# Reordering the transposes and the loads at the end of a block: two chunks among an output block, the last chunk behind it and copied by VectorE, x loads behind the output store

## Chip, cores, metric

One core of a Trainium2 chip. The metric is device microseconds of one execution. TensorE is called PE in the profile, VectorE DVE, ScalarE ACT, GpSimd POOL, SyncE SP.

## The reference

A softmax over seven taps weights a causal window of tokens (a dynamic convolution, 8 heads, group 24); its output goes through a two-layer block with the activation h - tanh(h):

```python
w = exp(weight_gen - max); w = w / (sum(w) + 1e-9)          # (8, 4096, 8, 7)
x_unf = x_pad[:, arange(S)[:, None] + arange(7)[None, :]]    # window of 7 tokens
x = einsum('bshk,bskhg->bshg', w, x_unf)                     # -> 32768 x 192
h = x @ w_in                                                 # 192 -> 2048
out = (h - tanh(h)) @ w_out                                  # 2048 -> 192
```

## The kernel before

It works through 32 blocks of 1024 tokens in a software pipeline. In block n, TensorE runs the first GEMM of block n (16 "f tiles": `gemm1`), the second GEMM of block n - 1 (8 output blocks `gemm2`, one behind each pair of f tiles) and, at the end, the transposes of the convolution of block n + 1 (matmuls with an identity that also add the taps). ScalarE takes the tanh, VectorE the subtraction, GpSimd the products of the convolution. Chunks are the thirds of the 192 channels (0, 1 and the last, 2); two row tiles take one half of the block's tokens each; "dense transposes" are the stretch in which most of TensorE's instructions are transposes; the halo is the six tokens before a block that the window needs, zeros at the head of a sequence. The code is cut:

```python
psum_h = ... bufs=3      # three double banks, one ring, tag "ph": f tiles and transposes
obank  = two single banks of the second GEMM

def gemm1(n, f):                       # one f tile
    ph = psum_h.tile([P, 2, HT], ...)  # next buffer of the ring
    ... 3 x 2 matmuls, two row tiles ...
    last_act[0] = nc.scalar.activation(out=th[:], in_=ph_f, func=ACT.Tanh)
    last_sub[0] = nc.vector.tensor_sub(gt[:], ph_f, th[:])   # frees ph
# ...
for n in range(NTOT):
    if n + 3 < NTOT and n not in LATE:
        load_x(n + 3)                              # head of the block
    for p in range(J):
        gemm1(n, 2 * p); gemm1(n, 2 * p + 1)
        # ... softmax sums in three parts, p = 1..3; reciprocals p = 4, 5
        if p < 6 or n == NTOT - 1:
            gemm2((n - 1) * J + p)                 # p = 0 also stores block n - 2
        # ...
    # end of the block: last chunk among output block 6, the other two behind it
    sums = conv_sums(n + 1, ((2,),), pcs)
    def between(f):
        if LEAD <= f: some(sums, mix)
        if f == LEAD + J - 1: conv_out(n + 1, ((2,),), pcs)      # ScalarE
    gemm2((n - 1) * J + 6, between=between)
    conv(n + 1, (0, 1))                                          # ScalarE copy
    gemm2((n - 1) * J + 7, 0, FILL)
    softmax_norm(n + 3, pcs[0][:, 0])     # VectorE: small copy, scale, in the last chunk's bank
    gemm1(n, 14)
    gemm2((n - 1) * J + 7, FILL, HALF)
    gemm1(n, 15)
    gemm2((n - 1) * J + 7, HALF, NFT)
```

"Tile 14" below is f tile 14 of a block, "tile 1" f tile 1 of the next block.

The softmax here doesn't subtract the row's maximum and nothing guards it: scores larger than these inputs give would overflow.

Of the kernel before, what the change touches and what calls it, by code (L numbers as in the profile page):

```python
# [16 lines left out]
def kernel(  # L17
# [8 lines left out]
    nc = tc.nc  # L26

    B, S, D = x.shape
    H, K = weight_gen.shape[2], weight_gen.shape[3]
# [3 lines left out]
    R = P // 2  # L33
    HALO = K - 1

    J = 8
    TOK = P * J
    JH = J // 2
    HT = TOK // 2
    NSB = S // TOK  # L40
    NTOT = B * NSB
    NFT = F // P
# [32 lines left out]
    prods_of = {}  # L75
# [27 lines left out]
    def load_x(n, behind=None):  # L103
        b, s = divmod(n, NSB)
        s0 = s * TOK

        x_t = xpool.tile([P, HALO + J, D], FP32, name="x_t")

        def rows(p0, p1, r0=0, r1=HALO + J):
            first = x[0, 0:1]  # L110
            return nc.sync.dma_start(
                out=x_t[p0:p1, r0:r1, :],
                in_=bass.AP(
                    tensor=first.tensor,
                    offset=first.offset + (b * S + s0 + p0 * J - HALO + r0) * D,
                    ap=[[J * D, p1 - p0], [D, r1 - r0], [1, D]],
                ),
            )

        def no_halo():  # L120
            nc.sync.dma_start(
                out=x_t[0:1, 0:HALO, :],
                in_=zero[:].rearrange("o (h d) -> o h d", h=1).to_broadcast([1, HALO, D]),
            )


        if n == 0:
            rows(0, P, HALO, HALO + J)
            rows(16, P, 0, HALO)
            rows(1, 16, 0, HALO)  # L130
            no_halo()
        else:
            dma = rows(0, P)
            if behind is not None:
                order(dma, behind, "order of the loads")
            if s == 0:

                no_halo()
        x_of[n] = x_t
# [11 lines left out]
    def softmax_sum(n, j0=0, j1=J):  # L151

        if j0 == 0:
            zsum_of[n] = wgpool.tile([P, J * H], FP32, name="zsum")
        nc.vector.reduce_sum(  # L155
            out=zsum_of[n][:, j0 * H : j1 * H],
            in_=e_of[n][:, j0:j1].rearrange("p j h k -> p (j h) k"),
            axis=AX.X,
        )
# [91 lines left out]
    def conv_sums(n, parts, pcs, home=None):  # L251


        prods = prods_of[n]
        if n not in conv_of:
            conv_of[n] = cpool.tile([P, NC, HT], BF16, name="convT")
        for _ in parts:
            pcs.append(home or psum_h.tile([P, 2, HT], FP32, name="pc", tag="ph"))

        for gi in range(max(len(g) for g in prods)):  # L260
            for chunks, pc in zip(parts, pcs):
                some = [c for c in chunks if gi < len(prods[c])]
                last = gi == max(len(prods[c]) for c in chunks) - 1
                for c in some:
                    for j in range(JH):
                        col = ((c - chunks[0]) * JH + j) * R
                        for r in range(2):
                            nc.tensor.matmul(  # L268
                                pc[r][:, col : col + R] if home else pc[:, r, col : col + R],
                                lhsT=prods[c][gi][  # L270
                                    r * R : (r + 1) * R, c, 2 * j : 2 * j + 2
                                ].rearrange("p j h g -> p (j h g)"),
                                rhs=ident[r * R : (r + 1) * R, r * R : (r + 1) * R],
                                start=(gi == 0 and c == chunks[0] and j == 0),
                                stop=(last and c == some[-1] and j == JH - 1),
                            )
                            yield

    def conv_out(n, parts, pcs):
        for chunks, pc in zip(parts, pcs):  # L280
            c0, nch = chunks[0], len(chunks)
            out = conv_of[n][:, c0 : c0 + nch, :].rearrange("p c (j r t) -> p r (c j) t", r=2, t=R)
            cols = nch * JH * R
            if isinstance(pc, list):
                for r in range(2):
                    nc.scalar.activation(  # L286
                        out=out[:, r],
                        in_=pc[r][:, 0:cols].rearrange("p (cj t) -> p cj t", t=R),
                        func=ACT.Copy,
                    )  # L290
            else:
                last_conv[0] = nc.scalar.activation(  # L292
                    out=out,
                    in_=pc[:, :, 0:cols].rearrange("p r (cj t) -> p r cj t", t=R),
                    func=ACT.Copy,
                )

    def conv(n, *parts):
        pcs = []
        for _ in conv_sums(n, parts, pcs):  # L300
            pass
        conv_out(n, parts, pcs)

    def gemm1(n, f):
        convT = conv_of[n]
        ph = psum_h.tile([P, 2, HT], FP32, name="ph", tag="ph")
        for c in range(NC):
            for r in range(2):
                nc.tensor.matmul(  # L309
                    ph[:, r, :],  # L310
                    lhsT=w_in[r * R : (r + 1) * R, c, f * P : (f + 1) * P],
                    rhs=convT[r * R : (r + 1) * R, c, :],
                    start=(c == 0),
                    stop=(c == NC - 1),
                )
        th = tpool.tile([P, TOK], FP32, name="th")
        ph_f = ph[:].rearrange("p r t -> p (r t)")
        g1_act[0] = last_act.get(0)
        gt = gpool.tile([P, TOK], BF16, name=f"gt{f}", tag=f"gt{f}")
        last_act[0] = nc.scalar.activation(out=th[:], in_=ph_f, func=ACT.Tanh)  # L320
        last_sub[0] = nc.vector.tensor_sub(gt[:], ph_f, th[:])  # L321
        g_of.setdefault(n, []).append(gt)

    LAST = (NTOT - 1) * J
    LATE = (1, 2, 3)
    LEAD = 5
    FILL, HALF = 2, 9
    half = {}
    out_of = {}

# [139 lines left out]
    def some(sums, m):  # L470
        for _ in range(m):
            next(sums, None)

    load_wg(3)
    load_wg(4)
    for n in range(NTOT):
        if n + 3 < NTOT and n not in LATE:
            load_x(n + 3)
        for p in range(J):
            gemm1(n, 2 * p)  # L480
            gemm1(n, 2 * p + 1)
            if n == 0:


                if p == 3:
                    pcs = []
                    sums = conv_sums(1, ((0, 1),), pcs, obank)
                if 3 <= p <= 6:
                    some(sums, (3 if p == 3 else 1) * 4 * JH)
                if p == 7:  # L490
                    some(sums, K * 4 * JH)
                    conv_out(1, ((0, 1),), pcs)
                    conv(1, (2,))
                continue
            if p == 0 and n == 1:
                softmax_exp(3)
            if p == 1 and n == 1:
                softmax_norm_ramp(3)
                products(3)
            if n + 3 < NTOT:  # L500

                if p == 0:
                    softmax_exp(n + 3)
                if p == 0 and n + 4 < NTOT:
                    load_wg(n + 4)
                if 1 <= p <= 3:
                    softmax_sum(n + 3, (p - 1) * 3, min(p * 3, J))
                if 4 <= p <= 5:
                    softmax_recip(n + 3, (p - 4) * JH, (p - 3) * JH)
            if p < 6 or n == NTOT - 1:  # L510
                gemm2((n - 1) * J + p)
            if p == 0 and 1 < n < NTOT - 2:
                products(n + 2, behind=last_sub[0])
            if p == 6 and n < NTOT - 1:
                break
        if not 1 <= n < NTOT - 1:
            continue


        pcs = []  # L520
        sums = conv_sums(n + 1, ((2,),), pcs)
        mix = len(prods_of[n + 1][2]) * 2 * JH // J

        def between(f):
            if LEAD <= f:
                some(sums, mix)
            if f == LEAD + J - 1:
                conv_out(n + 1, ((2,),), pcs)

        gemm2((n - 1) * J + 6, between=between)  # L530
        conv(n + 1, (0, 1))
        gemm2((n - 1) * J + 7, 0, FILL)
        if n + 3 < NTOT:

            softmax_norm(n + 3, pcs[0][:, 0])
        gemm1(n, NFT - 2)
        gemm2((n - 1) * J + 7, FILL, HALF)
        gemm1(n, NFT - 1)
        gemm2((n - 1) * J + 7, HALF, NFT)
        if n in LATE:  # L540


            load_x(n + 3, last_conv[0])
# [33 lines left out]
```

## Time and profile before

| | before |
|---|---|
| median of 4 runs (range) | 762.34 us (761.52 to 763.42) |
| period of a steady block, from start times in the trace | 22.637 us |
| TensorE's own work in it | 22.44 us |

The time was given first as 762.01 us, the median of three of these runs. Busy shares tell little here: TensorE is busy for 97%, and the ends of its matmuls are modelled. The prediction therefore reads start times: what the pieces of the chain of waits take, against what they take where nothing is in their way.

### The profile page before, as it was taken

The page shows a single profiled execution, that of the slowest core. Times are in us where ns is not written, and L with a number is a line of the kernel's source. Part 1 is how long each engine was busy: PE and PEld are TensorE (multiplying, and loading weights), DVE is VectorE, ACT ScalarE, POOL GpSimd, SP SyncE. Part 2 cuts the span into 40 slices and gives each one's busy share as a digit, 9 for nine tenths or more (in the row PEclk, how much of TensorE's full clock was granted, in tenths as well). Part 3 has the DMA queues.
Part 4 walks back from the last instruction along what each step waited for, and adds up shares of the span by engine and source line. Part 5 has one row for each costly group of instructions (what it writes and reads, how often), then busy time and mean ns, then how long its engine had stood idle before and what let it go on. Part 6 is the DMA issues. An engine that isn't in the chain of part 4 may idle for free.

```text
span 760.7 us, 32533 instructions
## 1 busy us (share of the span) xinstructions
PE 737.8 (97%) x14848; PEld 575.5 (76%) x14848; DVE 676.3 (89%) x737; ACT 642.3 (84%) x869; POOL 668.7 (88%) x262
## 2 busy tenths in 40 slices
PE   3799999999999999999999999999999999999997
PEld 2477777777778777777877777877777777777777
DVE  7988898989999999999999999998999999998893
ACT  4888888888888888888888888888888888888882
POOL 8999999999999999999999999999999999999000
PEclk9999999999999999999999999999999999999999
DMA  8903347576555775545775655666555577552212
GB/s 216 234 24 129 135 123 186 146 193 146 124 155 157 184 184 130 132 143 149 184 185 130 150 134 149 174 183 171 124 125 151 167 183 180 111 128 62 76 43 85
DMA packets 25399, 110.04 MB, mean 145 GB/s; under 512 B 4671, under 2 KB 9519, under 8 KB 21294
## 3 DMA queue, kind: packets, MB, share of 16 engines
q1 hardware_dynamic: 14718, 77.03, 28.5%
q0 software_dynamic: 10544, 30.94, 25.6%
q8 instruction: 116, 1.90, 1.0%
q14 instruction: 21, 0.17, 0.1%
HBM read 54.52 MB, written 25.17 MB: 105 GB/s over the span
## 4 chain that ended last, share of the span: by engine, by line
PE 93%; DVE 4%; DMA 1%; ACT 1%; issue 1%; ACTq 0%; DVEq 0%
PE obank L344 43%; PE ph L309 43%; PE pc L268 6%; DVE gt L321 3%; PE po L379 1%; DMA x_t<-in_x_dram 1%; DVE odd L220 0%; DMA wg_t<-in_weight_gen_dram 0%; DVE even L220 0%; ACT th L320 0%; DVE zsum L155 0%; ACT e_t L144 0%; DVE zr L164 0%; DVE wsm L194 0%; ACT convT L286 0%
## 5 line engine op out<-in xcount | busy, mean ns | idle before, releaser
L321 DVE TENSOR_TENSOR gt<-ph,th 128x1024 bf16<-128x1024 f32 x512 | 603.1, 1220 | 65.1 <-ACT th L320 61.3
L320 ACT ACTIVATE th<-ph 128x1024 f32<-128x1024 f32 x512 | 500.5, 1022 | 63.0 <-PE ph L309 57.9
L344 PE MATMUL obank<-w_out,gt 64*128 64x192 bf16 x7936 | 402.6, 243 | 1.9 <-issue 0.9
L309 PE MATMUL ph<-convT,w_in 64*128 64x512 bf16 x3072 | 391.3, 378 | 5.0 <-DVE gt L321 2.7
L344 PEld LDWEIGHTS <-gt 64*128 64x128 bf16 x7936 | 350.0, 94 | 59.6 <-issue 1.1
L220 POOL TENSOR_TENSOR even<-x_t,wsm 128x1536 bf16<-128x1536 f32 x93 | 275.2, 2959 | 22.6 <-DVE gt L321 22.4
L220 POOL TENSOR_TENSOR odd<-x_t,wsm 128x1536 bf16<-128x1536 f32 x93 | 275.0, 2957 | 0.0
L309 PEld LDWEIGHTS <-w_in 64*128 64x128 bf16 x3072 | 172.8, 94 | 107.2 <-issue 19.4
L220 POOL TENSOR_TENSOR last<-x_t,wsm 128x1536 bf16<-128x1536 f32 x32 | 105.9, 3308 | 0.0
L363 ACT ACTIVATE out_sb<-obank 128x192 f32<-128x192 f32 x248 | 81.7, 329 | 7.4 <-PE obank L344 3.1
L292 ACT ACTIVATE convT<-pc 128x512 bf16<-128x512 f32 (+1 forms) x63 | 50.7, 807 | 28.4 <-PE pc L268 28.4
L268 PE MATMUL pc<-ident,even 64*128 64x64 bf16 x2256 | 57.2, 191 | 1.2 <-issue 0.9
L268 PEld LDWEIGHTS <-even 64*128 64x128 bf16 x2304 | 54.2, 96 | 2.2 <-issue 1.3
L235 POOL DMA_DIRECT2D even<-odd x28 | 33.7, 1205 | 8.7 <-POOL odd L220 8.7
L268 PE MATMUL pc<-ident,last 64*128 64x64 bf16 x752 | 27.4, 191 | 9.3 <-POOL last L220 9.3
L155 DVE TENSOR_REDUCE zsum<-e_t 128x24 f32<-128x168 f32 (+2 forms) x88 | 27.5, 312 | 3.0 <-ACT e_t L144 3.0
L268 PEld LDWEIGHTS <-last 64*128 64x128 bf16 x768 | 20.2, 96 | 9.6 <-POOL last L220 9.3
L144 ACT ACTIVATE e_t<-wg_t 128x448 f32<-128x448 f32 x32 | 18.4, 578 | 7.3 <-DMA wg_t<-in_weight_gen_dram 7.3
L164 DVE RECIPROCAL zr<-zsum 128x32 f32<-128x32 f32 (+1 forms) x58 | 20.3, 350 | 0.1
L268 PE MATMUL pc<-ident,odd 64*128 64x64 bf16 x464 | 18.8, 197 | 1.7 <-POOL odd L220 0.7
L194 DVE TENSOR_TENSOR wsm<-e_t,pc 128x448 f32<-128x448 f32 x28 | 17.4, 622 | 2.9
L268 PEld LDWEIGHTS <-odd 64*128 64x128 bf16 x512 | 15.4, 99 | 2.5 <-POOL odd L220 0.9
(27 smaller groups left out, 64.3 us busy)
## 6 DMA issues: line engine op xcount, KB each, us to landing
x_t<-in_x_dram SPq DMA_DIRECT2D x31, 1344.0 KB, 9.4
even<-odd POOLq DMA_DIRECT2D x28, 1024.0 KB, 8.8
out_dram<-out_sb SPq DMA_DIRECT2D x31, 768.0 KB, 10.0
wg_t<-in_weight_gen_dram SPq DMA_DIRECT2D x32, 224.0 KB, 6.4
x_t<-in_x_dram SPq DMA_DIRECT2D x1, 768.0 KB
w_out<-in_moe_w_out_dram POOLq DMA_DIRECT2D x1, 768.0 KB, 9.2
out_dram<-out_sb SPq DMA_DIRECT2D x4, 192.0 KB, 1.8
x_t<-in_x_dram SPq DMA_DIRECT2D x1, 504.0 KB
```

The lines of the kernel that those rows point to most:

```text
L144: last_exp[0] = nc.scalar.activation(out=e_t[:].rearrange("p j h k -> p (j h k)"), in_=wg_t[:].rearrange("p j h k -> p (j h k)"), func=ACT ...
L155: nc.vector.reduce_sum(out=zsum_of[n][:, j0 * H : j1 * H], in_=e_of[n][:, j0:j1].rearrange("p j h k -> p (j h) k"), axis=AX.X,)
L164: nc.vector.reciprocal(zr_of[n][:, j0 * H : j1 * H], zsum_of[n][:, j0 * H : j1 * H])
L220: mul = eng.tensor_mul(dst[k][:, :, j0:j1].rearrange("p c j h g -> p j h c g"), x_t[:, k + j0 : k + j1, :].rearrange("p j (h c g) -> p j h ...
L235: nc.gpsimd.dma_start(out=even[:].rearrange("p i c j h g -> p (i c j h g)")[:, 0:ACC], in_=odd[:].rearrange("p i c j h g -> p (i c j h g)" ...
L268: nc.tensor.matmul(pc[r][:, col : col + R] if home else pc[:, r, col : col + R], lhsT=prods[c][gi][r * R : (r + 1) * R, c, 2 * j : 2 * j + ...
L292: last_conv[0] = nc.scalar.activation(out=out, in_=pc[:, :, 0:cols].rearrange("p r (cj t) -> p r cj t", t=R), func=ACT.Copy,)
L309: nc.tensor.matmul(ph[:, r, :], lhsT=w_in[r * R : (r + 1) * R, c, f * P : (f + 1) * P], rhs=convT[r * R : (r + 1) * R, c, :], start=(c == ...
L320: last_act[0] = nc.scalar.activation(out=th[:], in_=ph_f, func=ACT.Tanh)
L321: last_sub[0] = nc.vector.tensor_sub(gt[:], ph_f, th[:])
L344: mm = nc.tensor.matmul(po[:, 0:D], lhsT=g_of[n][f][r * R : (r + 1) * R, col : col + P], rhs=w_out[r * R : (r + 1) * R, f, :], start=(r == ...
L363: last_act[0] = nc.scalar.activation(out=out_sb[:, j, :], in_=po[:, 0:D], func=ACT.Copy)
```

## The change

Intent: the last chunk's copy leaves ScalarE, the big ScalarE copy starts earlier, VectorE's sums are done a pair of tiles sooner, and the output store does not sit behind an x load in the in-order SyncE queue. The core of the diff:

```diff
-    def conv_out(n, parts, pcs):
+    def conv_out(n, parts, pcs, eng=None):
+            elif eng is not None:
+                eng.tensor_copy(out, pc[:, :, 0:cols].rearrange("p r (cj t) -> p r cj t", t=R))
# ...
-        if n + 3 < NTOT and n not in LATE:
-            load_x(n + 3)                    # head of the block
# ...
-                if 1 <= p <= 3:
-                    softmax_sum(n + 3, (p - 1) * 3, min(p * 3, J))
-                if 4 <= p <= 5:
-                    softmax_recip(n + 3, (p - 4) * JH, (p - 3) * JH)
+                if 1 <= p <= 2:
+                    softmax_sum(n + 3, (p - 1) * JH, p * JH)
+                if 3 <= p <= 4:
+                    softmax_recip(n + 3, (p - 3) * JH, (p - 2) * JH)
# ...
+            if p == 0 and n + 3 < NTOT and n not in LATE:
+                load_x(n + 3)                # behind gemm2 of p = 0, which stores block n - 2
# ... end of the block
-        sums = conv_sums(n + 1, ((2,),), pcs)
-        gemm2((n - 1) * J + 6, between=between)
-        conv(n + 1, (0, 1))
-        gemm2((n - 1) * J + 7, 0, FILL)
+        sums = conv_sums(n + 1, ((0, 1),), pcs)
+        mix = -(-len(prods_of[n + 1][0]) * 2 * 2 * JH // (NFT - LEAD))
+        out_block(n, 6, between=lambda f: some(sums, mix if f >= LEAD else 0))
+        some(sums, K * 4 * JH)
+        conv_out(n + 1, ((0, 1),), pcs)
+        pcs = []
+        some(conv_sums(n + 1, ((2,),), pcs), K * 4 * JH)
+        out_block(n, 7, 0, 2)
+        conv_out(n + 1, ((2,),), pcs, nc.vector)
         softmax_norm(n + 3, pcs[0][:, 0])
-        gemm1(n, NFT - 2)
-        gemm2((n - 1) * J + 7, FILL, HALF)
-        gemm1(n, NFT - 1)
-        gemm2((n - 1) * J + 7, HALF, NFT)
+        gemm1(n, 14)
+        gemm1(n, 15)
+        out_block(n, 7, 2)
```

(`out_block(n, p, ...)` is `gemm2((n - 1) * J + p, ...)`; the rest of the diff moves block 0 out of the loop.)

More of the change, by code (lines that the diff above doesn't have):

```diff
@@ L324 @@
     LAST = (NTOT - 1) * J
+    LEAD = 5
     LATE = (1, 2, 3)
-    LEAD = 5
-    FILL, HALF = 2, 9
     half = {}
@@ L475, with out_block @@
     load_wg(4)
-    for n in range(NTOT):
-        if n + 3 < NTOT and n not in LATE:
-            load_x(n + 3)
+    load_x(3)
+    for p in range(J):
+        gemm1(0, 2 * p)
+        gemm1(0, 2 * p + 1)
+        if p == 3:
+            pcs = []
+            sums = conv_sums(1, ((0, 1),), pcs, obank)
+        if 3 <= p <= 6:
+            some(sums, (3 if p == 3 else 1) * 4 * JH)
+    some(sums, K * 4 * JH)
+    conv_out(1, ((0, 1),), pcs)
+    conv(1, (2,))
+    def out_block(n, p, f0=0, f1=NFT, between=lambda f: None):
+        gemm2((n - 1) * J + p, f0, f1, between)
+    for n in range(1, NTOT):
         for p in range(J):
+            more = n < NTOT - 1
+            if more and p == 6:
+                break
             gemm1(n, 2 * p)
             gemm1(n, 2 * p + 1)
-            if n == 0:
-                if p == 3:
-                    pcs = []
-                    sums = conv_sums(1, ((0, 1),), pcs, obank)
-                if 3 <= p <= 6:
-                    some(sums, (3 if p == 3 else 1) * 4 * JH)
-                if p == 7:
-                    some(sums, K * 4 * JH)
-                    conv_out(1, ((0, 1),), pcs)
-                    conv(1, (2,))
-                continue
             if p == 0 and n == 1:
@@ L505 @@
                     load_wg(n + 4)
-                if 1 <= p <= 3:
-                    softmax_sum(n + 3, (p - 1) * 3, min(p * 3, J))
-                if 4 <= p <= 5:
-                    softmax_recip(n + 3, (p - 4) * JH, (p - 3) * JH)
-            if p < 6 or n == NTOT - 1:
-                gemm2((n - 1) * J + p)
+                if 1 <= p <= 2:
+                    softmax_sum(n + 3, (p - 1) * JH, p * JH)
+                if 3 <= p <= 4:
+                    softmax_recip(n + 3, (p - 3) * JH, (p - 2) * JH)
+            out_block(n, p)
             if p == 0 and 1 < n < NTOT - 2:
                 products(n + 2, behind=last_sub[0])
-            if p == 6 and n < NTOT - 1:
-                break
-        if not 1 <= n < NTOT - 1:
+            if p == 0 and n + 3 < NTOT and n not in LATE:
+                load_x(n + 3)
+        if not more:
             continue
+        gemm1(n, 12)
+        gemm1(n, 13)
         pcs = []
-        sums = conv_sums(n + 1, ((2,),), pcs)
-        mix = len(prods_of[n + 1][2]) * 2 * JH // J
-        def between(f):
-            if LEAD <= f:
-                some(sums, mix)
-            if f == LEAD + J - 1:
-                conv_out(n + 1, ((2,),), pcs)
-        gemm2((n - 1) * J + 6, between=between)
-        conv(n + 1, (0, 1))
-        gemm2((n - 1) * J + 7, 0, FILL)
+        sums = conv_sums(n + 1, ((0, 1),), pcs)
+        mix = -(-len(prods_of[n + 1][0]) * 2 * 2 * JH // (NFT - LEAD))
+        out_block(n, 6, between=lambda f: some(sums, mix if f >= LEAD else 0))
+        some(sums, K * 4 * JH)
+        conv_out(n + 1, ((0, 1),), pcs)
+        pcs = []
+        some(conv_sums(n + 1, ((2,),), pcs), K * 4 * JH)
+        out_block(n, 7, 0, 2)
+        conv_out(n + 1, ((2,),), pcs, nc.vector)
         if n + 3 < NTOT:
             softmax_norm(n + 3, pcs[0][:, 0])
-        gemm1(n, NFT - 2)
-        gemm2((n - 1) * J + 7, FILL, HALF)
-        gemm1(n, NFT - 1)
-        gemm2((n - 1) * J + 7, HALF, NFT)
+        gemm1(n, 14)
+        gemm1(n, 15)
+        out_block(n, 7, 2)
         if n in LATE:
```

## The prediction

> **What bounds the kernel now.** I read the busy shares first, then the chain of work that ended last, then one steady block in order of time, last the instructions' stretches without work.
>
> ```profile
> PE 737.8 (97%) x14848; PEld 575.5 (76%) x14848; DVE 676.3 (89%) x737; ACT 642.3 (84%) x869; POOL 668.7 (88%) x262
> ...
> PE 93%; DVE 4%; DMA 1%; ACT 1%; issue 1%; ACTq 0%; DVEq 0%
> ```
>
> TensorE carries 93% of the chain; four engines are above 84%, so any can become a wait. A busy TensorE may still lose time, so I read the chain inside one block of 1024 tokens (start us, us, what):
>
> ```profile
> 405.90 1.47 PE ph L309 x12
> 407.37 1.32 PE obank L344 x32
> 408.69 1.29 PE ph L309 x12
> ...
> 424.71 0.25 PE obank L344 x6
> 424.96 0.93 PE pc L268 x64
> 425.89 0.17 PE obank L344 x4
> 426.06 0.68 PE ph L309 x6
> 426.73 0.58 PE obank L344 x14
> 427.31 0.65 PE ph L309 x6
> ...
> 428.54 1.47 PE ph L309 x12
> ```
>
> Twelve first-GEMM matmuls (six pairs of row tiles) take 1.29 to 1.30 us, 216 ns a pair; 32 second-GEMM matmuls 1.32 us, 82.5 ns a pair; 64 transposes 0.93 us, 14.5 ns each. Sixteen f tiles of three pairs are 48 x 0.216 = 10.37 us, 128 pairs of the second GEMM 10.56, the 104 transposes (64 for chunks 0 and 1, 40 for chunk 2) 1.51: together 22.44 us. The 1.47 us piece comes back after 428.54 - 405.90 = 22.64 us. So TensorE loses only 0.20 us a block. Two places show it: 1.47 instead of 1.30 at the first pair of f tiles (0.17), and 0.68 instead of 0.65 at f tile 14 (0.03). That bounds what reordering can bring: 0.20 x about 30 blocks = 6 us, 0.8%.
>
> Who holds these two places? The timeline at the end of the block (start, us, engine, line):
>
> ```profile
> 423.50 2.36 DVE L321 TENSOR_TENSOR gt<-ph,th 128x1024 bf16<-128x1024 f32 x2
> ...
> 425.24 0.33 ACT L363 ACTIVATE out_sb<-obank 128x192 f32<-128x192 f32 x1
> ...
> 425.91 0.82 PE L309 MATMUL ph<-convT,w_in 64*128 64x512 bf16 x6
> 425.93 1.02 ACT L292 ACTIVATE convT<-pc 128x1024 bf16<-128x1024 f32 x1 [0.36 <-PE pc L268]
> ...
> 426.85 2.17 ACT L320 ACTIVATE th<-ph 128x1024 f32<-128x1024 f32 x2
> ...
> 427.90 1.22 DVE L321 TENSOR_TENSOR gt<-ph,th 128x1024 bf16<-128x1024 f32 x1 [1.18 <-ACT th L320]
> ```
>
> The three double-bank PSUM buffers go round: f tile 14 takes the one that subtraction 13 frees, at 423.50 + 2.36 = 425.86, and f tile 1 of the next block the one that subtraction 14 frees, at 427.90 + 1.22 = 429.12. Tile 14 ends near 426.74, but its tanh starts at 426.85 because ScalarE is copying two chunks from 425.93 on. That delay reaches tile 1, which starts near 429.18.
>
> A second, irregular loss: TensorE now and then waits for nothing that the profile shows. Waits of two windows, and the SyncE queue's issues in the blocks of both:
>
> ```profile
> PEld L268 <- issue: 0.6, 1, 0.6
> ...
> PEld L344 <- issue: 1.1, 1, 1.1
> ```
> ```profile
> 108.44 10.49 SPq L111 DMA_DIRECT2D x_t<-in_x_dram  x2
> ...
> 120.52 1.17 SPq L367 DMA_DIRECT2D out_dram<-out_sb  x1
> ...
> 149.09 0.70 SPq L121 DMA_DIRECT2D x_t<-zero  x1
> ...
> 150.38 0.36 SPq L367 DMA_DIRECT2D out_dram<-out_sb  x1
> ```
>
> They lie at 129 and 153 us; two of 0.15 and 0.17 us follow at 516 and 606. In all four blocks the output store went out late, behind an x load or its zeroed halo.
>
> **What the skill says.** "TensorE: Matmul & The Clock Gate", section "Wait — 56ns, not 53.3ns?": a warm matmul costs N / 2.4 GHz + about 2.5 ns; that is 82.5 ns at N = 192 and 215.8 at 512, what the trace has. So the two GEMMs are at their floor. "VectorE: DVE Perf Modes", "Mode 2×_2P": the two-port mode needs SBUF, PSUM has one read port; so the new VectorE copy out of PSUM runs at one element a cycle. No such copy is in the trace; the two sizes of sum, 168 inputs in 317 ns and 112 in 259, give 1.04 ns an element. "SBUF — State Buffer", "Who interferes with whom": outside two-port modes, a VectorE instruction with at most one SBUF input does not block GpSimd; I take the copy as harmless to GpSimd. No run shows that yet. "Runtime: NRT & Kernel Launch", "Instruction fetch mechanics": instructions arrive in blocks of 16 KiB, 256 instructions. The page's 116 packets of 1.90 MB agree (16.4 KB each), and counting TensorE's loads and matmuls up to the four issue waits gives 189, 188, 172 and 168 modulo 256, nearly one place: late refills, during dense transposes and mostly behind busy DMA.
>
> **The change, part by part.**
> (a) Order on TensorE. Nothing is added or removed: 64 transposes (two chunks) go six per f tile among the output block from f = 5 (64 / 6, rounded up, is 11 f tiles: f = 5 to 15), then 40 of the last chunk, two f tiles of output, f tiles 14 and 15 back to back, 14 f tiles of output. The sum stays 22.44 us. Output block 6 starts at 422.87; f = 5 ends 0.495 us later, 11 times (82.5 + 6 x 14.5) ns end near 425.13, 40 x 14.5 ns at 425.71, two output pairs at 425.88: tile 14 is ready at the same time as now and waits the same 0.03 us for subtraction 13.
> (b) ScalarE. The 598 ns copy of one chunk leaves it. The output block's copy starts near 425.29 (its last matmul starts at 425.01, takes 243 ns, 40 ns to be seen), the two-chunk copy near 425.60, and ends at 426.62. The tanh of tile 14 can then start when the tile is complete, 426.77, not 426.85: 0.08 us won.
> (c) A new wait. The ring of PSUM buffers turns: tile 15 now takes the buffer of the two chunks and follows tile 14 at once. It would start at 425.91 + 0.65 = 426.56, but the buffer is free at 426.62 + 0.05 = 426.67: 0.11 us lost. The built program shows this wait of tile 15 on ScalarE, where before it waited for VectorE.
> (d) Tile 1 of the next block. TensorE arrives at 426.67 + 0.65 + 14 x 0.0825 + 0.65 = 429.12. Subtraction 14 starts at 426.77 + 1.02 + 0.03 = 427.82, ends at 429.05, seen at 429.10: no wait. Before 429.18, now 429.12: **0.055 us a block**, over 28 such blocks (the chain has its piece of 1.40 to 1.47 us in nearly every block from 110 to 723 us) 1.5 us.
> (e) VectorE. The new copy is about 218 ns (the copy of 64 elements) + 448 x 1.04 = 0.68 us, from 425.93 (transposes ended) to 426.61; the small copy 0.22 and the scale 0.62 follow to 427.5, still 0.3 us before subtraction 14 can start. It fits in the 1.18 us that VectorE idles there. Sums in two parts of 32 instead of three: 317 + 56 x 1.04 = 375 ns, 30 ns more than the 344 ns between subtractions; twice 30 ns against a slack near 0.06 us: nothing, or some ns.
> (f) The SyncE queue. Store first, then x load, which waits for GpSimd to free its buffer until 409.1 anyway. The store no longer waits for the halo; the DMA peaks move away from the dense transposes. Of the four issue waits (0.67 + 1.09 + 0.15 + 0.17 = 2.1 us) I count 1.4 as gone.
> (g) Blocks 1 to 3, with seven tap groups: 56 last-chunk transposes give ScalarE 0.23 us more, so no new wait; 0.1 us each, 0.3 us. Ramp and tail are unchanged.
> Sum: 1.5 + 1.4 + 0.3 = 3.2 us: 762.0 - 3.2 = **758.8 us**.
>
> **The rivals.** (1) The new wait grows: if ScalarE's two-chunk copy ends 0.1 us later than I place it, tile 15 and all behind it slip, 0.05 us worse than before: 28 x 0.05 = +1.4, time near 761 to 763. For it: ScalarE has two copies and no gap there. Against: its copies start 40 ns after their releaser all over the trace. (2) VectorE becomes the bound: a copy of 1.0 us or the longer sums delay subtraction 14 or the mid-block ones; a 0.1 us stall a block is +3 us, 763 to 765. Against: 0.3 us of room. (3) TensorE is at its floor and the issue waits are only moved to other refills: gain 1.5 us or less, 760.5. For it: early refill waits at 59 and 83 us came with idle DMA, by dense transposes alone, and their density stays. (4) All 0.20 us is won: 756. Against it, the loop of tile 14, tanh, subtraction, tile 1 takes 0.87 + 1.05 + 1.28 = 3.20 us from tile 14's start, TensorE's own work between 3.10, so 0.10 stays in one form or another.
>
> **Range and chances.** The rivals span 756 to 764; the runs of before span 1.9 us. I take 755.8 to 762.4. Over 2% faster needs 746.8 us, which is below the floor of the matmuls plus ramp: 0.01. Over 2% slower needs 0.5 us of new stall in every block: 0.02. Within 2%: 0.97.
>
> **What would show it.** A block period of 22.58 us instead of 22.64; the first pair of f tiles in 1.30 instead of 1.47; a gap of 0.1 us ahead of tile 15, released by the ScalarE copy; the VectorE copy near 0.68 us; tanh 14 starting 0.08 us earlier; output stores within a few us of the block's start in every block; no issue waits at 129 and 153. A period of 22.64 or more, subtraction 14 behind the scale, or issue waits in other blocks would make the prediction wrong.

## More of the kernel before

Granted TensorE clock is 0.997 to 1.000, except in four of the six runs of the kernel with the useless load (0.992 to 0.994) and in three single runs of others (0.995, 0.996, 0.996).

## The result, and the profile after

758.86 us, median of 4 runs (758.62 to 759.39), against 762.34. The ratio is the mean time of one kernel's fast runs over that of the other's of the same rounds, so not quite the ratio of the medians: 0.9954, 95% interval 0.9937 to 0.9972. Faster by about half a per cent; within 2%.

The chain of waits of the changed kernel, one block (start us, us, what):

```profile
403.93 1.37 PE ph L311 x12
405.30 1.32 PE obank L345 x32
406.62 1.30 PE ph L311 x12
...
423.19 0.64 PE pc L268 x44
423.83 0.17 PE obank L345 x4
424.00 1.35 PE ph L311 x12
425.35 1.16 PE obank L345 x28
426.50 1.37 PE ph L311 x12
```

The piece that took 1.47 us takes 1.37, and comes back after 426.50 - 403.93 = 22.57 us instead of 22.64. Tiles 14 and 15, now in one piece, take 1.35 where 1.30 is the floor. Start times in the trace place what is left, per block: tile 14 waits 0.03 us, tile 15 0.027, tile 1 0.076; together 0.13 us where 0.20 stood.

The timeline of the same block's end, the answer to the one that the prediction shows:

```profile
421.44 2.36 DVE L323 TENSOR_TENSOR gt<-ph,th 128x1024 bf16<-128x1024 f32 x2 [0.26 <-ACT th L322]
...
423.23 0.33 ACT L364 ACTIVATE out_sb<-obank 128x192 f32<-128x192 f32 x1 [0.90 <-PE obank L345]
...
423.45 1.02 ACT L294 ACTIVATE convT<-pc 128x1024 bf16<-128x1024 f32 x1
...
423.85 1.50 PE L311 MATMUL ph<-convT,w_in 64*128 64x512 bf16 x12
423.87 0.69 DVE L292 CAST convT<-pc 128x512 bf16<-128x512 f32 x1
...
424.71 1.94 ACT L322 ACTIVATE th<-ph 128x1024 f32<-128x1024 f32 x2 [0.24 <-PE ph L311]
424.93 0.62 DVE L194 TENSOR_TENSOR wsm<-e_t,pc 128x448 f32<-128x448 f32 x1
...
425.77 2.36 DVE L323 TENSOR_TENSOR gt<-ph,th 128x1024 bf16<-128x1024 f32 x2 [0.22 <-ACT th L322]
```

The tanh of tile 14 starts 424.71 - 423.85 = 0.86 us after the tile, and what it waits for is now TensorE ("<-PE ph"); before, it was 426.85 - 425.91 = 0.94 us, and ScalarE was busy with the copy. The new VectorE copy (its row is named CAST) lies in VectorE's idle stretch and ends at 424.56, before that tanh starts.

The SyncE queue around 150 us: the store does not wait for the zeroed halo any more, so it is 14 us earlier than the 150.38 of before.

```profile
136.09 0.34 SPq L368 DMA_DIRECT2D out_dram<-out_sb  x1
140.09 0.33 SPq L111 DMA_DIRECT2D x_t<-in_x_dram  x1
150.32 0.70 SPq L121 DMA_DIRECT2D x_t<-zero  x1
151.08 0.43 SPq L97 DMA_DIRECT2D wg_t<-in_weight_gen_dram  x1
159.01 0.34 SPq L368 DMA_DIRECT2D out_dram<-out_sb  x1
```

TensorE's irregular waits ("issue"), 126 to 156 us, first before, then after:

```profile
PEld L344 <- issue: 1.1, 1, 1.1
...
PEld L268 <- issue: 0.6, 1, 0.6
```
```profile
PEld L345 <- issue: 0.4, 1, 0.4
```

One is gone, the other fell from 1.1 to 0.4. And the busy shares of two stretches, before and after (the columns: stretch, its length, busy time and number of instructions of TensorE, its loads, VectorE, ScalarE, GpSimd, then granted clock, DMA share, GB/s):

```profile
126.00:128.00 2.00, 2.00 (x52) 1.56 (x48) 2.00 (x4) 1.68 (x3) 2.00 (x2) 1.00 0.91 336
...
152.00:154.00 2.00, 1.35 (x78) 1.18 (x70) 1.90 (x4) 1.51 (x3) 2.00 (x2) 1.00 0.90 368
```
```profile
126.00:128.00 2.00, 2.00 (x47) 1.54 (x45) 1.74 (x3) 1.68 (x3) 2.00 (x2) 1.00 0.31 111
...
152.00:154.00 2.00, 1.76 (x59) 1.12 (x53) 1.79 (x4) 1.33 (x3) 2.00 (x2) 1.00 0.41 115
```

The DMA engines, over 90% busy in these two stretches, where dense transposes begin or run, are at 31 and 41% there.

Adding up the two profiles from 100 to 735 us by start times: regular waits at f tiles 5.48 us before, 3.62 after; irregular waits 2.11 before, 0.80 after. Together 3.2 us less, and the span went from 760.7 to 757.6 us, 3.1 less.

### The profile page after: what moved, and what is told of

It reads as the page before. It is cut to its first block, busy times and chain, and to the rows that moved or that the text cites. A ratio compares the mean times of both kernels' runs of the same rounds, so it can differ in the third digit from the quotient of the medians.

```text
span 757.6 us, 32477 instructions
## 1 busy us (share of the span) xinstructions
PE 735.7 (97%) x14848; PEld 576.2 (76%) x14848; DVE 695.7 (92%) x739; ACT 625.1 (83%) x839; POOL 668.8 (88%) x262
## 4 chain that ended last, share of the span: by engine, by line
PE 93%; DVE 4%; DMA 1%; ACT 1%; issue 1%; ACTq 0%; DVEq 0%
PE obank L345 43%; PE ph L311 43%; PE pc L268 6%; DVE gt L323 2%; PE po L380 1%; DMA x_t<-in_x_dram 1%; DVE odd L220 0%; ACT th L322 0%; DMA wg_t<-in_weight_gen_dram 0%; DVE zsum L155 0%; DVE even L220 0%; ACT e_t L144 0%; DVE zr L164 0%; DVE wsm L194 0%; ACT convT L286 0%
## 5 line engine op out<-in xcount | busy, mean ns | idle before, releaser
L345 PE MATMUL obank<-w_out,gt 64*128 64x192 bf16 x7936 | 406.9, 243 | 1.2 <-ACT th L322 0.6
L311 PE MATMUL ph<-convT,w_in 64*128 64x512 bf16 x3072 | 384.1, 378 | 4.8 <-DVE gt L323 2.8
L268 PE MATMUL pc<-ident,even 64*128 64x64 bf16 x2256 | 64.0, 191 | 1.0 <-issue 0.8
L268 PEld LDWEIGHTS <-even 64*128 64x128 bf16 x2304 | 59.8, 96 | 1.8 <-issue 1.0
L294 ACT ACTIVATE convT<-pc 128x1024 bf16<-128x1024 f32 (+1 forms) x33 | 32.7, 993 | 2.6 <-PE pc L268 2.6
L268 PEld LDWEIGHTS <-last 64*128 64x128 bf16 x768 | 23.2, 96 | 9.4 <-POOL last L220 9.2
L292 DVE CAST convT<-pc 128x512 bf16<-128x512 f32 x30 | 20.8, 692 | 6.0 <-PE pc L268 4.0
L155 DVE TENSOR_REDUCE zsum<-e_t 128x32 f32<-128x224 f32 (+1 forms) x60 | 23.5, 392 | 2.9 <-ACT e_t L144 2.9
```

What stands on the lines that cost most here:

```text
L155: nc.vector.reduce_sum(out=zsum_of[n][:, j0 * H : j1 * H], in_=e_of[n][:, j0:j1].rearrange("p j h k -> p (j h) k"), axis=AX.X,)
L268: nc.tensor.matmul(pc[r][:, col : col + R] if home else pc[:, r, col : col + R], lhsT=prods[c][gi][r * R : (r + 1) * R, c, 2 * j : 2 * j + ...
L292: eng.tensor_copy(out, pc[:, :, 0:cols].rearrange("p r (cj t) -> p r cj t", t=R))
L294: last_conv[0] = nc.scalar.activation(out=out, in_=pc[:, :, 0:cols].rearrange("p r (cj t) -> p r cj t", t=R), func=ACT.Copy,)
L311: nc.tensor.matmul(ph[:, r, :], lhsT=w_in[r * R : (r + 1) * R, c, f * P : (f + 1) * P], rhs=convT[r * R : (r + 1) * R, c, :], start=(c == ...
L345: mm = nc.tensor.matmul(po[:, 0:D], lhsT=g_of[n][f][r * R : (r + 1) * R, col : col + P], rhs=w_out[r * R : (r + 1) * R, f, :], start=(r == ...
```

## The experiments

Twelve runs, one of them the changed kernel again. Two things were to be settled. First, whether the regular gain is that of one loop (tile 14, its tanh, its subtraction, tile 1), as the prediction has it, or of single waits. Second, whether the irregular waits are late instruction refills that DMA traffic makes later. "Period" and "irregular" come from the start times of each kernel's one profile; irregular waits are those among transposes and second-GEMM matmuls, from 100 to 735 us:

| kernel | median us | ratio to before, 95% | period us | irregular us |
|---|---|---|---|---|
| before | 762.34 | 1 | 22.637 | 2.1 |
| changed | 758.86 | 0.9954 (0.9937 to 0.9972) | 22.566 | 0.8 |
| changed, again | 759.63 | 0.9966 (0.9945 to 0.9987) | 22.563 | 0.7 |
| changed, loads at the head | 762.42 | 0.9966 (0.9942 to 0.9991) | 22.566 | 3.8 |
| before, loads behind the store | 761.69 | 0.9968 (0.9949 to 0.9987) | 22.638 | 1.1 |
| changed, ScalarE copies all | 763.38 | 0.9987 (0.9968 to 1.0006) | 22.711 | 0.5 |
| before, VectorE copies last chunk | 769.32 | 1.0065 (1.0044 to 1.0085) | 22.833 | 4.0 |
| changed, tile 15 apart | 760.03 | 0.9963 (0.9942 to 0.9983) | 22.563 | 0.4 |
| changed, tile 14 in halves | 774.08 | 1.0152 (1.0128 to 1.0175) | 23.075 | 0.3 |
| changed, tiles 12 and 14 in halves | 795.36 | 1.0429 (1.0405 to 1.0453) | 23.804 | not separable |
| changed, half tanh (wrong result) | 758.05 | 0.9931 (0.9907 to 0.9955) | 22.493 | 1.1 |
| changed, three sums | 760.90 | 0.9966 (0.9946 to 0.9985) | 22.564 | 1.3 |
| changed, useless load | 778.75 | 1.0196 (1.0171 to 1.0222) | 22.56 in the undisturbed half of the blocks | 10.6, and 5.4 at f tiles |
| before, late loads to block 5 | 765.43 | 1.0024 (1.0001 to 1.0047) | 22.637 | 3.1 |

The kernel before had medians of 764.27, 762.15 and 763.08 us in the three groups of runs, on their chips; so times of different groups are compared by their ratios only. Periods repeat within 0.003 us.

### The two parts apart: order of the transposes, and who copies

**Order of the change, all copies on ScalarE.**

```diff
-        conv_out(n + 1, ((2,),), pcs, nc.vector)
+        conv_out(n + 1, ((2,),), pcs)
```

> The changed kernel with the last chunk copied by ScalarE again: the new order of the transposes without the VectorE copy. Theory (chain from f tile 14 through its tanh and subtraction to tile 1 of the next block): both copies now stand ahead of the tanh of tile 14, which starts 0.16 us later than in the changed kernel; tile 1 waits about 0.24 us in place of 0.08; block period 22.72 to 22.75 us, time 763.3 to 764 us, slower than before. Rival (the gain comes from the order of the transposes, and the copy is indifferent because ScalarE has idle time elsewhere): 758.9 within 0.5.

763.38 us, the foretold time, but beside a kernel before of 764.27 us on that chip: by the times it cannot be told from before (0.9987, interval to 1.0006). The moved loads of the change are in it too, and its irregular waits are 0.5 us against 2.1, so the period has to decide. The period is 22.711, with the wait of tile 1 at 0.22 us by start times. Timeline of a block's end:

```profile
425.40 1.51 ACT L294 ACTIVATE convT<-pc 128x1024 bf16<-128x1024 f32 x2
...
426.78 1.97 ACT L322 ACTIVATE th<-ph 128x1024 f32<-128x1024 f32 x2
426.94 0.23 DVE L170 COPY pc<-zr 128x64 f32<-128x64 f32 x1 [1.20 <-ACT convT L294]
427.27 0.62 DVE L194 TENSOR_TENSOR wsm<-e_t,pc 128x448 f32<-128x448 f32 x1
427.86 4.69 DVE L323 TENSOR_TENSOR gt<-ph,th 128x1024 bf16<-128x1024 f32 x4
```

Both copies stand ahead of the tanh, and the scale, which uses the last chunk's bank, waits for the second of them as well; the subtraction of tile 14 (427.86) follows both. Without the VectorE copy the new order alone makes the steady block 0.07 us longer than before. The loop theory stands, its rival falls.

**Order as before, last chunk copied by VectorE.**

```diff
# ... conv_out takes an engine, as in the change
             if f == LEAD + J - 1:
-                conv_out(n + 1, ((2,),), pcs)
+                conv_out(n + 1, ((2,),), pcs, nc.vector)
```

> The kernel before with only the last chunk's copy given to VectorE; order of the transposes as before. Theory: ScalarE is relieved by 0.6 us, but the last-chunk buffer, in which the scale follows the copy, is the one that f tile 15 takes next; copy 0.69, small copy 0.23 and scale 0.62 end near 427.4 in the block that I followed, 0.3 us after tile 15 could start (427.13): a new wait of 0.3 us in every block, period near 22.9 us, time 767 to 770 us. Rival (ScalarE's load is what counts): the tanh of tile 14 starts earlier and the time is about that of the changed kernel, 759 to 760 us.

769.32 us. Relieving ScalarE by 0.6 us a block made the kernel slower, as the place in the ring had said:

```profile
430.03 0.68 DVE L292 CAST convT<-pc 128x512 bf16<-128x512 f32 x1
...
430.75 0.23 DVE L170 COPY pc<-zr 128x64 f32<-128x64 f32 x1
431.08 0.62 DVE L194 TENSOR_TENSOR wsm<-e_t,pc 128x448 f32<-128x448 f32 x1
...
431.76 0.82 PE L311 MATMUL ph<-convT,w_in 64*128 64x512 bf16 x6 [0.19 <-DVE wsm L194]
```

Tile 15 takes the last chunk's buffer, and VectorE keeps it until the scale is done. By start times tile 15 waits 0.365 us in nearly every block; the last line's 0.19 is the part of it in which TensorE's row is empty, since modelled ends cover the rest. So the new order and the VectorE copy each lengthen the steady block alone (22.711 and 22.833 against 22.637 us) and shorten it together (22.566): the order moves the buffer that VectorE holds longest to a later user (tile 0 of the next block instead of tile 15).

### Is it one loop?

**Tile 15 put back among the output block.**

```diff
         gemm1(n, 14)
+        out_block(n, 7, 2, 9)
         gemm1(n, 15)
-        out_block(n, 7, 2)
+        out_block(n, 7, 9)
```

> The changed kernel with f tile 15 put back among the output block's matmuls. Theory (the loop from tile 14 through tanh and subtraction to tile 1 of the next block is longer than TensorE's work in it, by a fixed amount): the wait of 0.03 us ahead of tile 15 goes, the wait ahead of tile 1 grows from 0.076 to about 0.10 us; period 22.57, time within 0.3 us of the changed kernel. Rival (the waits are separate, each is a loss of its own): period 22.54 us, 0.8 us faster.

760.03 us, 0.4 from the changed kernel's 759.63 on the same chip (within 0.3 was foretold; its own runs span 1.4 us); period 22.563 in both. The wait ahead of tile 15 is gone, the one ahead of tile 1 is 0.099 us, the sum of the two of the changed kernel within 0.003. The waits are one sum, not two losses.

**Half the tanh of tile 14 (wrong result).**

```diff
-        last_act[0] = nc.scalar.activation(out=th[:], in_=ph_f, func=ACT.Tanh)
-        last_sub[0] = nc.vector.tensor_sub(gt[:], ph_f, th[:])
+        b = HT if half_th else TOK                 # half_th: f == 14
+        last_act[0] = nc.scalar.activation(out=th[:, 0:b], in_=ph_f[:, 0:b], func=ACT.Tanh)
+        # subtraction at full length; for tile 14 the half tanh is read twice
```

> Wrong result on purpose: the changed kernel with the tanh of f tile 14 taken over one half of the tokens only (the subtraction uses that half twice, at its full length), so that ScalarE's step in the loop from tile 14 to tile 1 shrinks by about 0.45 us and nothing else changes or is added. Theory: VectorE can then start the subtraction when the scale has ended, 0.2 us earlier, and the 0.076 us ahead of tile 1 vanish; 0.03 ahead of tile 14 and 0.03 ahead of tile 15 stay; period 22.49 us, 28 x 0.076 = 2.1 us faster than the changed kernel, 757 us. Rival (tile 1 waits for another thing than this loop): tile 1 still waits 0.076 us, 759.3 us.

The wait ahead of tile 1 is gone, those of 0.03 and 0.027 us ahead of tiles 14 and 15 stay, and the period is 22.493 us: 0.073 less, as expected. 758.05 us, against 760.90 for the three-sums kernel beside it on the same chip, whose period is the changed kernel's. By the periods 28 x 0.071 = 2.0 us of these 2.85 are the loop's; the irregular waits of the two differ by 0.2 us in their profiles, and the rest is not accounted for. The tanh fell from 1026 to 597 ns and the subtraction stayed (1225 and 1218 ns), so ScalarE's step alone was shortened. What sets tile 1 is the loop, and taking time out of ScalarE's step in it shortened every block.

**Tile 14 in two halves, and tiles 12 and 14.** A correct way to the same end was tried:

```diff
-        th = tpool.tile([P, TOK], FP32, name="th")
# ...
-        last_act[0] = nc.scalar.activation(out=th[:], in_=ph_f, func=ACT.Tanh)
-        last_sub[0] = nc.vector.tensor_sub(gt[:], ph_f, th[:])
+        cut = 1 <= n < NTOT - 1 and f in (14,)          # (12, 14) in the second kernel
+        for a, b in ((0, HT), (HT, TOK)) if cut else ((0, TOK),):
+            th = tpool.tile([P, TOK], FP32, name="th")
+            last_act[0] = nc.scalar.activation(out=th[:, 0 : b - a], in_=ph_f[:, a:b], func=ACT.Tanh)
+            last_sub[0] = nc.vector.tensor_sub(gt[:, a:b], ph_f[:, a:b], th[:, 0 : b - a])
```

> The changed kernel with f tile 14's tanh and subtraction each cut into two halves, so that the first subtraction starts under the second tanh. Theory: the loop from tile 14 to tile 1 becomes about 0.14 us shorter (VectorE can start only when the scale has ended, 0.2 us before it starts now), more than the 0.076 us that tile 1 waits; that wait goes, 0.03 + 0.03 stay, period 22.49 us, 28 blocks x 0.076 = 2.1 us faster than the changed kernel: 756.8 us. Rival (tile 1 waits for something else, or two more instructions cost what they save): no gain, 758.9 or slower.

> As the kernel before it in this list, with f tile 12 cut into halves as well: tile 14 waits 0.03 us for subtraction 13, which follows 12. Theory: subtraction 12 starts 0.2 us earlier but both halves take 0.15 us more than one; subtraction 13 ends some 0.05 us earlier; the 0.03 us ahead of tile 14 go, period 22.46 us, 0.8 us faster than with tile 14 alone: 756.0. Rival (VectorE, now with two more instructions in its fullest stretch, becomes the bound): slower than with tile 14 alone.

Both missed: 774.08 and 795.36 us, slower by 1.5 and 4.3%. The timeline of the first:

```profile
432.78 0.60 ACT L324 ACTIVATE th<-ph 128x512 f32<-128x512 f32 x1 [0.24 <-PE ph L311]
...
433.53 0.68 DVE L325 TENSOR_TENSOR gt<-ph,th 128x512 bf16<-128x512 f32 x1
434.25 1.51 ACT L324 ACTIVATE th<-ph 128x512 f32<-128x512 f32 x2 [0.88 <-DVE gt L325]
434.88 0.69 DVE L325 TENSOR_TENSOR gt<-ph,th 128x512 bf16<-128x512 f32 x1 [0.66 <-ACT th L324]
435.62 0.82 PE L311 MATMUL ph<-convT,w_in 64*128 64x512 bf16 x6 [0.41 <-DVE gt L325]
```

The second tanh did not run under the first subtraction but waited for its end (433.53 + 0.68 = 434.21, start 434.25). The built program carries a wait of the second tanh on VectorE; I had it before me and took it for one that is long met. Which dependence put it there was not tested. The tanh pool has three buffers (`bufs=3`), so the second half does not take the buffer that the first subtraction reads; the PSUM tile, which both halves read, is left as a suspect. So these two do not test what they were made for; that halves which truly overlap would gain is left open. They still say something: the longer loop put the wait of tile 1 at 0.585 us, 0.51 more than in the changed kernel, and the period grew by as much (23.075 - 22.566 = 0.51). With tile 12 cut as well, tile 14 waits 0.70 us and tile 1 0.55 us: the same wait twice.

**Sums in three parts again.**

```diff
-                if 1 <= p <= 2:
-                    softmax_sum(n + 3, (p - 1) * JH, p * JH)
-                if 3 <= p <= 4:
-                    softmax_recip(n + 3, (p - 3) * JH, (p - 2) * JH)
+                if 1 <= p <= 3:
+                    softmax_sum(n + 3, (p - 1) * 3, min(p * 3, J))
+                if 4 <= p <= 5:
+                    softmax_recip(n + 3, (p - 4) * JH, (p - 3) * JH)
```

> The changed kernel with the softmax sums in three parts and the reciprocals one pair of f tiles later, as before. Theory (VectorE has 0.06 us of room per pair of tiles, and the block's end is not bound by it): no new gap in the middle of the block, waits ahead of tiles 14, 15 and 1 within 0.01 us of the changed kernel, time within 0.4 us of it. Rival (the freed sixth pair is what lets subtraction 13 end in time): tile 14 waits longer than 0.03 us, +1 us or more.

Period 22.564, the three waits of the block's end within 0.004 us of the changed kernel's. This part of the change does nothing that can be seen. 760.90 us has the ratio 0.9966 of the changed kernel's second measurement.

### The irregular waits

The prediction takes refills to come in blocks of 256 instructions; late ones should then show at one place of a block. Counting TensorE's weight loads and matmuls up to each irregular wait of over 0.1 us in blocks 1 to 30, modulo 256: 191 at 60 and 84 us in every kernel counted, 188 or 189 at 129 and 153, 172 near 515, 165 near 675; the value drifts evenly with the index, presumably because some instructions are not counted. Of the 66 such waits in thirteen kernels (the one with two tiles in halves, which has a regular wait at the transposes, was not counted) one is off this line: it lies behind the wait of 3.2 us, in 3.4 us in which the granted clock was 0.5, and is no refill. The others sit at one place of a 256-instruction block.

The traces hold the refills themselves. The page before lists

```profile
q8 instruction: 116, 1.90, 1.0%
```

and TensorE's loads and matmuls are 2 x 14848 = 116 x 256, one packet for 256 of them. Each of the 65 waits on the line, 0.1 to 3.2 us long, ended 1.2 to 1.6 us after the end of a packet of this queue. Where TensorE passed the same place without a wait (1363 times, the places taken from the line), the packet had ended 3.6 us before, in the median. After TensorE has come to one such place (counted from 0.3 us before it), the next packet starts 0.5 us later (median of 684) where other transfers keep the DMA engines under 20% busy in the following microsecond, and 3.3 us later (median of 553) where over 90%. So these waits are late refills, and DMA traffic goes with their lateness; the experiments below change the traffic.

**The changed kernel with the x loads at the head of the block.**

```diff
     for n in range(1, NTOT):
+        if n + 3 < NTOT and n not in LATE:
+            load_x(n + 3)
         for p in range(J):
# ...
-            if p == 0 and n + 3 < NTOT and n not in LATE:
-                load_x(n + 3)
```

> The changed kernel with the x loads at the head of the block again, ahead of the output store. Theory (late instruction refills follow the DMA peaks that this order makes): the steady block keeps its 22.57 us, and issue waits of TensorE at the dense transposes grow back, above all in the blocks whose store waits for a zeroed halo: +1.0 us, 759.9 us. Rival (refill waits follow the number of dense transposes alone, and the order of the loads is worth nothing): 758.9 within 0.4, with issue waits of the same total as in the changed kernel (about 0.8 us beyond 100 us).

The profile has the two waits back at 130 and 154 us, larger than before: 1.40 and 2.18 us, 3.8 us in all, and the steady period of the changed kernel. The time does not decide it: runs from 759.95 to 763.56 us, ratio 0.9966 with an interval that holds both expectations (759.9 and 758.9 us would be 0.997 and 0.996).

**The kernel before with the x loads behind the store.**

```diff
-        if n + 3 < NTOT and n not in LATE:
+        if n == 0:
             load_x(n + 3)
# ...
                 products(n + 2, behind=last_sub[0])
+            if p == 0 and n + 3 < NTOT and n not in LATE:
+                load_x(n + 3)
```

> The kernel before with only the x loads moved behind the output store. Theory: the steady block keeps 22.64 us (tile 1 of the next block still 0.17 us late), the issue waits beyond 100 us shrink from 2.1 to about 0.8 us: 761.1 us, a gain of 1.0 to 1.3. Rival (load order worth nothing): 762.3 within 0.4.

Ratio 0.9968, clear of 1: this part of the change gains by itself, 0.3%, or 2.4 us (1.0 to 3.9 by the interval) where 1.0 to 1.3 was foretold. The period is that of before, the irregular waits 1.1 us: nothing at 129, 0.30 at 154. The two gains do not simply add up (0.32% here, 0.34% with the loads at the head, 0.34 and 0.46% for both); with intervals of 0.2% each way, that cannot be settled by the times.

**A useless load of the same size in every block.**

```diff
+            if more and p == 4 and n > 3:
+                dma = nc.sync.dma_start(out=idle[:], in_=<1.3 MB of x>)
+                order(dma, last_sub[0], "idle traffic")
             out_block(n, p)
```

> The changed kernel with one useless load of 1.3 MB (the size of an x load) in each block from the fourth on, issued in the fifth pair of f tiles, so that the DMA engines are busy during the dense transposes. Theory (instruction refills come late when the DMA engines are busy while the transposes use up instructions fast): issue waits of 0.3 to 2 us at or right behind the transposes in a third to a half of the blocks, +5 to +20 us. Rival (the refill waits have nothing to do with DMA traffic, or the other traffic's own delays are what counts): issue waits as in the changed kernel, below 1 us in all, time within 1 us of it.

778.75 us, 2% slower than before. Irregular waits of 10.6 us beyond 100 us, at 223, 268, 359, 430, 521, 596 and 686 us, with one of 3.2; and four more that fall inside f tiles 14, 15 and 0 just behind the transposes, at 312, 385, 476 and 641 us (2.09, 0.21, 1.36 and 1.69 us), at the same place modulo 256 and 1.4 to 1.5 us behind a packet's end:

```profile
PEld L268 <- issue: 6.2, 3, 3.2
PEld L345 <- issue: 6.0, 7, 1.8
PE pc L268 <- issue: 5.9, 3, 3.1
PE ph L311 <- issue: 4.4, 3, 1.9
```

That is eleven of the 27 blocks with the load, the third to a half that was foretold, with sizes of 0.2 to 3.2 us (0.3 to 2 foretold). Together they are 16 us, 14.7 more than in the three-sums kernel on the same chip, and the spans of the two profiles differ by as much (774.0 and 759.3 us). That the two agree so well is in part luck: the 3.4 us at half clock behind the longest wait are a loss of their own, and a block with such a wait can save a regular one. The lower granted clock of the other runs (0.992 to 0.994 in four, 0.997 in the profiled one, the fastest of the six) may be part of their longer times. Still, traffic that does nothing else brings such waits, at the same place modulo 256, and they account for the loss in the profile.

**Only the loads of blocks 4 and 5 moved, in the kernel before.**

```diff
-    LATE = (1, 2, 3)
+    LATE = (1, 2, 3, 4, 5)
```

> The kernel before with the x loads of blocks 4 and 5 alone issued at the end of the block, as those of blocks 1 to 3 are. Theory (the load order pays in blocks 4 and 5, where the two large issue waits lie): these two waits, 0.67 and 1.09 us in the profile, go or fall below 0.5 us together; steady period 22.64 as before; 1.2 us faster than before or more. Rival (the waits at 129 and 153 us are chance, and turn up elsewhere): no gain against before.

A miss in time: 765.43 us, 0.24% slower. The waits at 129 and 153 us did vanish, but one of 2.27 us came at 198. The SyncE queue and the DMA share suggest why:

```profile
189.69 0.33 SPq L111 DMA_DIRECT2D x_t<-in_x_dram  x1
190.06 1.38 SPq L97 DMA_DIRECT2D wg_t<-in_weight_gen_dram  x1
191.54 0.89 SPq L367 DMA_DIRECT2D out_dram<-out_sb  x1
```
```profile
196.00:198.00 2.00, 2.00 (x91) 2.00 (x87) 2.00 (x4) 1.64 (x3) 2.00 (x2) 1.00 0.95 221
198.00:200.00 2.00, 0.65 (x46) 0.53 (x37) 1.60 (x3) 0.55 (x2) 2.00 (x2) 1.00 1.02 400
```

The late loads held GpSimd up (it waited 6.4 us for a zeroed halo once), the x load of the next block went out at 189.7 us, and its store at 191.5 behind it, so the DMA engines were full at the dense transposes again (95 to 102% at 196 to 200 us). The wait had been moved, not removed: what counts here is that the traffic and a refill within the transposes do not meet, not which block it is in.

**The changed kernel once more.**

> The changed kernel itself once more, on the chip of the next three kernels. Theory: period 22.57 us, 758.9 us, and runs within about 1 us of each other, against up to 5 us among runs of the kernel before, whose late refills vary. Rival (the spread is the chip's): the same spread as the kernel before.

759.63 us, ratio 0.9966; the period repeats. The six runs spread over 2.6 us (759.06 to 761.66), against 4.6 us for eleven runs of before beside them (more runs also spread wider); I had expected about 1 us, a miss. Refills remain (0.49 us at 155, 0.25 at 516), so the change made them smaller in the profiles and did not end them.

## Why the prediction was right, point by point

- **Bound and floor.** Right. TensorE's GEMMs stand at 216 and 82.5 ns a pair, and only 0.20 us a block could be won; 0.07 was.
- **(a), the order on TensorE.** Right: the same work, 14.4 to 14.6 ns a transpose among the output block as behind it. One product is written wrongly: "11 times" gives 425.23; ten pairs of the output block and 64 transposes behind f = 5 give 425.12, which is what the next step uses.
- **(b), ScalarE.** Right: the tanh of tile 14 starts 0.08 us earlier relative to its tile, released by TensorE.
- **(c), the new wait of tile 15.** Its mechanism was right, its size off: 0.11 foretold, 0.027 measured. The mis-sized term is the distance between ScalarE's two copies. I took 0.31 us from the start of the output copy to that of the chunk copy; it was 423.45 - 423.23 = 0.22, since the second copy starts before the first, of 0.33 us, has ended. The trace before showed such overlap: two tanhs of 1.02 us in 1.94.
- **(d), the wait of tile 1.** It was foretold as gone; 0.076 us stayed. The loop's excess over TensorE's work is waited for once, at tile 15 or at tile 1; with a shorter wait at tile 15, more of it was left for tile 1. The prediction's rival (4) had the sum: the loop takes 3.20 us, TensorE's work 3.10, "0.10 stays in one form or another"; 0.027 + 0.076 = 0.103. The kernel with tile 15 apart shows that it is one sum. So the gain was 0.070 us a block, not 0.055: 1.9 us instead of 1.5.
- **(e), VectorE.** Right: the copy took 692 ns (foretold 684) and delayed nothing; the longer sums cost nothing that shows.
- **(f), the SyncE queue.** Right in kind and nearly in size: 1.3 us fewer irregular waits in the one pair of profiles, 1.4 foretold. Of the two large waits foretold as gone, the one at 129 us went and the one at 153 stayed with 0.42 us. The kernel before with this part alone is faster by 0.3%. But waits of this kind vary from run to run, so the agreement of the number is partly luck.
- **(g), blocks 1 to 3.** Waits at f tiles fell from 0.70 to 0.56 us by start times, less than the 0.3 us foretold, and the refill waits at 59 and 83 us, which rival (3) named, stayed (1.28 before, 1.55 after).

The sum of 3.2 us was met by 3.1 us of span because the steady gain was larger and the ramp's smaller than foretold. That 758.8 met 758.86 so closely is luck: the same kernel had a median of 759.63 us on another chip. GpSimd's products were not disturbed by the copy, as the prediction took it: 2.90 us in the stretch of the copy as beside it.

## What to carry to other kernels

When an engine is at its floor, add up the regular waits per period by start times before judging a reordering; here that capped the gain at 0.8% and named the loop to shorten. A buffer ring decides who may take over an evacuation: here, moving work to an idle engine helped only together with the order that gives its buffer to the latest user, and hurt by 0.65% alone. Keep bulk DMA away from the stretches where TensorE uses up instructions fastest (here two loads and two matmuls in 29 ns), and look again after each move, since the traffic can meet the next such stretch.

## What the Trainium skill lacked or had wrong

- "Runtime: NRT & Kernel Launch", "Instruction fetch mechanics": it calls the cost of crossing a 16 KiB boundary "mostly hidden" and says nothing of DMA traffic. Most crossings here cost nothing that shows; but in or right behind dense transposes (two loads and two matmuls in 29 ns) 65 of about 1430 in thirteen kernels cost more than 0.1 us, up to 2.3 us, and 3.2 us with extra traffic. It gives no time for a refill: here TensorE went on 1.2 to 1.6 us after the end of the packet.
- "TensorE: Matmul & The Clock Gate", "Wait — 56ns, not 53.3ns?": start-to-start "never drops below" about 25 ns. The section does not say that this is for one row tile. With two row tiles in turn, transposes of 64 columns start 20 and 9 ns apart; each tile has one every 29.1 ns, which is the page's N / 2.4 GHz + 2.5 ns at N = 64.
- Nothing wrong was found in the two other pages cited. "VectorE: DVE Perf Modes", "Mode 2×_2P": a copy out of PSUM has no two-port mode; 512 fp32 elements to bf16 in SBUF took 692 ns, about 1.06 ns for each element beyond the 64-element copy's 218 ns. "SBUF — State Buffer", "Who interferes with whom": GpSimd's products stayed at 2.90 us beside this copy.
